# One rotation of eight PSUM banks, and another order of products and output matmuls, in an attention and gMLP kernel

## The chip, the cores and the metric

The kernel runs on one core of a Trainium2 chip. The metric is device time in microseconds for one execution. TensorE multiplies matrices into PSUM, which has eight banks. VectorE, ScalarE and GpSimd do the work between the matmuls, and SyncE's queue issues the DMA transfers.

## The reference

Three parts follow one another. Attention with a causal window of 128 over 4 batches, 8 heads, 576 positions and head size 64 gives `x`. A gated MLP with a spatial gate turns `x` into a new `x`, and a gated linear unit with a depthwise convolution ends it.

```python
scores = scale * q @ k.T + bias          # window 128, slopes by head
attn = exp(scores - max) / sum           # then attn @ v -> x [4, 576, 512]

h = gelu(x @ w_in)                       # 512 -> 1024
u, v = h[..., :512], h[..., 512:]
v_n = (v - mean) / sqrt(var + 1e-6) * g_ln
v_s = einsum('ts,bsd->btd', w_sg, v_n) + b_sg
x = x + (u * v_s) @ w_out                # spatial gate, back to 512

h = relu(x @ w_in)
gate = sigmoid(depthwise_conv(h, 3))
return (h * gate) @ w_out
```

## The kernel before

The program is one string of steps, built by `_steps()`, and each step is a function that emits instructions on several engines. A tile scheduler then orders each engine's queue by these steps, and a planner (`pick`, `book`, the table `load`) chooses for each piece of helper work the engine that it expects to be free first. TensorE's work in the two middle parts runs through the helper `mm` (L213), transpositions through L515.

Batches 0 to 2 run in a software pipeline: while the gMLP of batch b is computed, the attention of batch b + 1 is worked in between. In one such round come first the V and U steps of batch b (`psv`, `psu`: the matmuls with `w_in`), and then the second half of the round, which the change touches. Its steps, where p counts pairs of heads of the next batch:

- `C` scores of a pair (`sc`, five PSUM banks), `E` the score additions on VectorE (L451, tiles `t`, `st`) and the exponentials on ScalarE (L186), nine of each, `N` the reciprocal `r` of the sums (L498, L499) and nine norms (L242).
- `T` thirteen transpositions of a pair's weights into four banks (`pT`) and their copies to `ph` (L222 on ScalarE, L224 on VectorE), `A` 52 matmuls of the products with V (`o`), `X` the copies of the products to `x` and their two-part split into `xg`.
- `G` the spatial gate: 14 matmuls `pss` for each of eight groups, the eviction `t` (L840, VectorE), the product with `u` (L231, GpSimd) and the split into `gh` and `gl`.
- `W` the output matmuls `pso`, 12 for each of eight groups, with the sum `x` of `pso` and the old `x` (L231), which is stored to `x2d` by SyncE (L859). The buffers of the eviction `t` and of this stored sum come from one pool, so either can wait for a store to land.
- `a` pieces of narrowing a later weight (`wa`, L324 to L331, `wh`), woven into batches 1 and 2.

Each of the names `T`, `A`, `G[0]` (256 columns), `G[1]` (320 columns), `W[0]`, `W[1]` in the code is a list with one entry for each pair or group, and `gw` is the order of the second half. PSUM's eight banks are two pools until batch 3: two banks for all `ps` names except `pT` (the network) and six for `sc`, `pT` and `o` (attention); the helper `bank` takes the next in turn. The function `one_rotation` makes one pool of all eight; it is a step named `B`, which before doesn't use. Batch 3 and the last part have banks of their own.

Of the kernel before, what the change touches and what calls it, by code (L numbers as in the profile page):

```python
# [14 lines left out]
B, H, S, D = 4, 8, 576, 64  # L15
# [38 lines left out]
def _steps():  # L54


    def of(p):
        return f"{p // NP}.{p % NP}"

    def scores(p):  # L60
        return [f"C{of(p)}"]

    def weigh(p):
        return [f"E{of(p)}", f"N{of(p)}"]
# [4 lines left out]
    def halves(p):  # L69
        return [f"X{of(p)}.0", f"X{of(p)}.1"]  # L70

    def loads(p):
        return [f"L{of(p)}", f"M{of(p)}"]
# [5 lines left out]
    s = """  # L79
# [6 lines left out]
    for b in range(B - 1):  # L86
        p = NP * (b + 1)
        V = [f"V{b}.{j}" for j in range(5)]
        U = [[f"U{b}.{half}.{m}" for m in range(4)] for half in range(2)]
        G = [[f"G{b}.{half}.{m}" for m in range(4)] for half in range(2)]  # L90
        W = [[f"W{b}.{half}.{m}" for m in range(4)] for half in range(2)]
        if b == 0:
            uv = ["g0", "g1", V[2], "g2", "o0.0", U[0][3], "g3", "o0.1", V[4]] + loads(p) + ["g4", "o1.0"] + scores(p) + ["o1.1", V[3], "o2.0", "o2.1"]
            uv += loads(p + 1) + U[1][:2] + ["o3.0"] + scores(p + 1) + ["o3.1"] + loads(p + 2) + U[1][2:] + scores(p + 2)
        else:
            uv = V[:2] + loads(p) + scores(p) + V[2:] + loads(p + 1) + scores(p + 1) + U[0] + loads(p + 2) + U[1][:1] + scores(p + 2) + U[1][1:]
        T, A = ([f"{x}{of(p + i)}" for i in range(4)] for x in "TA")
        gw = weigh(p) + G[0] + weigh(p + 1) + G[1][:1] + loads(p + 3) + T[:1] + G[1][1:2] + W[0][:1] + A[:1] + halves(p)
        gw += weigh(p + 2) + W[0][1:2] + T[1:2] + W[0][2:] + A[1:2] + scores(p + 3) + halves(p + 1) + weigh(p + 3) + T[2:3] + G[1][2:3]
        gw += A[2:3] + halves(p + 2) + G[1][3:] + T[3:] + W[1][:1] + A[3:] + halves(p + 3) + W[1][1:]  # L100
        if b == 0:
            s += uv + gw
        else:
            now = put_by[10 * b - 10 : 10 * b]
            s += weave(uv, now[:4]) + weave(gw, now[4:])
# [11 lines left out]
    s = weave(n[:-6], put_by[LATE:]) + n[-6:]  # L117
    late = [f"w1.{k}.{h}" for k in range(4) for h in range(2)]
    s = s[:-6] + weave(s[-6:], late)
# [996 lines left out]
```

## Time and profile before

| what | us |
|---|---|
| median of 3 runs | 545.88 |
| lowest and highest run | 544.2, 546.34 |
| the profiled execution | 545.05 |
| its span | 543.2 |
| TensorE busy in it | 522.3 |
| VectorE busy | 370.0 |
| ScalarE busy | 258.6 |
| GpSimd busy | 243.0 |

The span runs from the first to the last instruction. Of the profiled span, 82 to 126.1 is about the second half of batch 0's round, 126.1 to 157.3 the V and U steps of batch 1, 157.3 to 205.5 batch 1's second half, 205.5 to 238 batch 2's V and U steps, 238 to 284.9 its second half; batch 3 and the last part follow. A row of a timeline reads: start, length, engine, line, operation, result and operands, count, and in brackets the idle time ahead of it and what ended it. TensorE's rows overlap a little, since its matmuls are pipelined. "PEclk" is the share of TensorE's full clock that was granted.

### The profile page before, as it was taken

The numbers are of one execution on the slowest core, as the hardware profiler recorded it, in microseconds if no ns is written. First come the engines' busy times: TensorE is split into PE (matmuls) and PEld (weight loads), VectorE is DVE, ScalarE is ACT, GpSimd is POOL, SyncE is SP. The second block draws the span as 40 slices with busy tenths as digits, with TensorE's granted clock in tenths as the row PEclk, the third lists the DMA queues.
The fourth block names the chain that finished last, engine by engine and source line by source line (L and its number), as shares of the span: only waits on it lengthen the run. The fifth ranks groups of instructions, "written<-read, shape, count | busy, mean of one in ns | idle before, by whom it ended". The sixth has DMA issues, their size and how long they took to land.

```text
span 543.2 us, 11985 instructions
## 1 busy us (share of the span) xinstructions
PE 522.3 (96%) x4548; PEld 474.8 (87%) x4548; DVE 370.0 (68%) x959; ACT 258.6 (48%) x673; POOL 243.0 (45%) x383
## 2 busy tenths in 40 slices
PE   8997989999999999999999999999999999999997
PEld 6776879898898888898988999998998999999887
DVE  4999898754869865869867788698467344654300
ACT  6694578342458451457544534453444334444311
POOL 2444249552246263237363354245586445465500
PEclk9999989999999999999999999999999999999999
DMA  8974441433260766240734424811202200100111
GB/s 298 385 241 172 150 126 45 146 120 106 80 194 21 229 183 198 68 136 24 241 124 131 154 80 155 306 43 43 83 21 69 77 21 19 42 21 22 37 39 59
DMA packets 33209, 63.93 MB, mean 118 GB/s; under 512 B 3968, under 2 KB 13952, under 8 KB 33152
## 3 DMA queue, kind: packets, MB, share of 16 engines
q1 hardware_dynamic: 33008, 63.04, 35.0%
q8 instruction: 36, 0.59, 0.4%
q14 instruction: 21, 0.17, 0.1%
q10 hardware_dynamic: 144, 0.13, 0.1%
HBM read 48.47 MB, written 14.68 MB: 116 GB/s over the span
## 4 chain that ended last, share of the span: by engine, by line
PE 57%; DVE 17%; ACT 11%; POOL 8%; DMA 3%; issue 3%; ACTq 0%; POOLq 0%; DVEq 0%; SPq 0%
PE psg L213 31%; PE pso L213 7%; PE psu L213 5%; ACT t L186 5%; PE psv L213 4%; PE o L213 3%; PE sc L213 3%; POOL t L242 3%; PE pss L213 3%; DVE t L451 2%; PE pT L515 2%; DMA x2d<-x 2%; DVE t L242 1%; DVE wa L330 1%; DVE wa L329 1%
## 5 line engine op out<-in xcount | busy, mean ns | idle before, releaser
L213 PEld LDWEIGHTS psg<-x2g,w 128*128 128x128 f32 x768 | 103.2, 188 | 2.4 <-ACT hb L970 0.7
L213 PE MATMUL psg<-x2g,w 128*128 128x256 f32 (+1 forms) x768 | 104.7, 294 | 0.6 <-ACT hb L970 0.5
L213 PE MATMUL psg<-wout,gh 128*128 128x512 f32 (+1 forms) x272 | 80.1, 378 | 0.0
L186 ACT ACTIVATE t<-t,st 128x192 f32<-128x192 f32 (+1 forms) x144 | 61.9, 431 | 16.6 <-DVE st L451 16.6
L213 PE MATMUL pss<-wsg,vn 128*128 128x256 f32 (+1 forms) x448 | 63.6, 299 | 0.3 <-DVE t L840 0.2
L213 PEld LDWEIGHTS pss<-wsg,vn 128*128 128x128 f32 x448 | 60.7, 191 | 1.2 <-DVE t L840 1.1
L974 DVE SCALAR_TENSOR_TENSOR cc<-hb,cw,cc 128x576 f32<-128x576 f32 x32 | 26.5, 832 | 47.0 <-POOL cc L242 47.0
L213 PEld LDWEIGHTS psg<-wout,gh 128*128 128x128 f32 x272 | 49.7, 188 | 8.7
L213 PE MATMUL psu<-xg,win 128*128 128x320 f32 (+1 forms) x384 | 54.4, 298 | 3.0 <-ACT win L222 1.7
L213 PEld LDWEIGHTS psu<-xg,win 128*128 128x128 f32 x384 | 51.6, 188 | 4.3 <-ACT win L222 1.8
L213 PE MATMUL pso<-gh,wo 128*128 128x256 f32 (+1 forms) x256 | 52.2, 300 | 1.7 <-DVE t L840 1.6
L213 PE MATMUL psg<-wout,gl 128*128 128x512 f32 (+1 forms) x136 | 50.9, 378 | 0.0
L213 PE MATMUL psv<-win,xg 128*128 128x512 f32 x192 | 47.6, 398 | 1.0 <-DVE wa L328 0.9
L242 POOL TENSOR_SCALAR cc<-hb,cw 128x576 f32<-128x576 f32 x32 | 28.4, 889 | 42.7 <-ACT hb L970 42.7
L451 DVE CUSTOM_DVE_ANT_0 t<-sc,tab 128x192 f32<-128x192 f32 (+1 forms) x144 | 40.3, 335 | 4.9 <-PE sc L213 4.9
L970 ACT ACTIVATE hb<-psg 128x576 f32<-128x576 f32 x32 | 20.7, 651 | 47.5 <-PE psg L213 45.1
L213 PEld LDWEIGHTS pso<-gh,wo 128*128 128x128 f32 x256 | 40.2, 188 | 3.4 <-DVE t L840 2.8
L213 PEld LDWEIGHTS psv<-win,xg 128*128 128x128 f32 x192 | 35.4, 188 | 8.9 <-ACT win L222 1.0
L231 DVE TENSOR_TENSOR gg<-cc,hb 128x576 f32<-128x576 f32 x32 | 30.2, 944 | 17.2 <-ACT cc L186 17.0
L213 PE MATMUL pso<-gl,wo 128*128 128x256 f32 (+1 forms) x128 | 36.9, 301 | 2.4 <-DVE gl L231 1.7
L231 POOL TENSOR_TENSOR t<-t,u 128x256 f32<-128x256 f32 (+1 forms) x32 | 27.0, 850 | 21.3 <-DVE t L840 20.3
L231 POOL TENSOR_TENSOR gl<-gg,gh 128x512 fp32r<-128x512 f32 x24 | 33.7, 1406 | 0.6
(101 smaller groups left out, 963.1 us busy)
## 6 DMA issues: line engine op xcount, KB each, us to landing
V<-in_v_dram SPq DMA_DIRECT2D x12, 704.0 KB, 5.1
x2s<-x2d SPq DMA_DIRECT2D x16, 288.0 KB, 2.9
w<-in_w_in_dram SPq DMA_DIRECT2D x8, 512.0 KB, 7.4
w<-in_w_out_dram SPq DMA_DIRECT2D x16, 256.0 KB, 2.9
w<-in_w_in_dram SPq DMA_DIRECT2D x16, 256.0 KB, 2.7
wout<-w2d SPq DMA_DIRECT2D x8, 512.0 KB, 6.1
q<-in_q_dram SPq DMA_DIRECT2D x12, 320.0 KB, 3.9
out_dram<-ot SPq DMA_DIRECT2D x15, 256.0 KB, 2.0
```

Of the source, the lines that this page charges most:

```text
L186: ins = nc.scalar.activation(*args, **kw)
L213: return nc.tensor.matmul(out, lhsT, rhs, start=start, stop=stop, **kw)
L231: return (nc.vector if eng == "dve" else nc.gpsimd).tensor_tensor(dst, a, b, op=op)
L242: e.tensor_scalar(dst, src, col, 1.0, op0=ALU.mult, op1=ALU.mult)
L329: nc.vector.tensor_scalar(a, a, 0x07FFFFFF, 3, op0=ALU.bitwise_and, op1=ALU.logical_shift_left)
L330: nc.vector.scalar_tensor_tensor(a, high, 0xC0000000, a, op0=ALU.bitwise_and, op1=ALU.bitwise_or)
L451: nc.vector.tensor_tensor_reduce(e, bank, table, scale=-SCALE, scalar=3e38, op0=ALU.add, op1=ALU.min, accum_out=mx)
L515: grouped(nc.tensor.transpose(ps[:, i * P : (i + 1) * P], src, ident), first and i == 0, waits if i == 0 else ())
L970: nc.scalar.activation(h[:, 1 : S + 1], ps[:, 256 : 256 + S], AF.Relu)
L974: nc.vector.scalar_tensor_tensor(cc, h[:, 0:S], cw[:, 0, c : c + 1], cc, op0=ALU.mult, op1=ALU.add)
```

## The change

A step `B` is put after batch 0's V and U steps, so all eight banks form one rotation from batch 0's second half to batch 2. And `gw` is written anew: the first group of `pso` (`W[0][:1]`) goes from ahead of the first pair's products to behind the third pair's weights (`weigh(p + 2)`), so that the products (`A[:1]`) follow `pss` directly; the third transpositions (`T[2:3]`) go ahead of the last scores, and their products ahead of the last two groups of `pss` instead of behind the first of them; the last group of `W[0]` goes from ahead of the last scores to behind these `pss` groups; the last weights (`weigh(p + 3)`) go behind the third products. The first three lines of `gw` stay in the code, overwritten.

```diff
--- before.py
+++ after.py
@@ -98,8 +98,12 @@
         gw = weigh(p) + G[0] + weigh(p + 1) + G[1][:1] + loads(p + 3) + T[:1] + G[1][1:2] + W[0][:1] + A[:1] + halves(p)
         gw += weigh(p + 2) + W[0][1:2] + T[1:2] + W[0][2:] + A[1:2] + scores(p + 3) + halves(p + 1) + weigh(p + 3) + T[2:3] + G[1][2:3]
         gw += A[2:3] + halves(p + 2) + G[1][3:] + T[3:] + W[1][:1] + A[3:] + halves(p + 3) + W[1][1:]
+        if True:
+            gw = weigh(p) + G[0] + weigh(p + 1) + G[1][:1] + loads(p + 3) + T[:1] + G[1][1:2] + A[:1] + halves(p)
+            gw += weigh(p + 2) + W[0][:1] + T[1:2] + W[0][1:2] + A[1:2] + halves(p + 1) + T[2:3] + W[0][2:3] + scores(p + 3)
+            gw += A[2:3] + halves(p + 2) + weigh(p + 3) + G[1][2:] + W[0][3:] + T[3:] + W[1][:1] + A[3:] + halves(p + 3) + W[1][1:]
         if b == 0:
-            s += uv + gw
+            s += uv + ["B"] + gw
         else:
             now = put_by[10 * b - 10 : 10 * b]
             s += weave(uv, now[:4]) + weave(gw, now[4:])
```

In after all line numbers behind the diff are higher by four (L217 for L213, L519 for L515, L844 for L840).

The first place is TensorE's queue in batch 1, at the first pair's products `o`. Before:

```order
L213 MATMUL pso<-gh,wo 128x256 x2
L213 MATMUL pso<-gl,wo 128x256
L213 MATMUL o<-ph,V 64x64 x4
L213 MATMUL o<-ph,V 64x192 x2
L213 MATMUL o<-ph,V 64x64 x16
L213 MATMUL o<-ph,V 64x128 x2
L213 MATMUL o<-ph,V 64x64 x2
L515 MATMUL pT<-ident,t_86 128x128 x13
L213 MATMUL pso<-gh,wo 128x256 x2
```

After:

```order
L217 MATMUL pss<-wsg_851,vn 128x320 x2
L217 MATMUL pss<-wsg_852,vn 128x320
L217 MATMUL o<-ph,V 64x64 x4
L217 MATMUL o<-ph,V 64x192 x2
L217 MATMUL o<-ph,V 64x64 x16
L217 MATMUL o<-ph,V 64x128 x2
L217 MATMUL o<-ph,V 64x64 x2
L217 MATMUL pso<-gh,wo 128x256
L519 MATMUL pT<-ident,t_86 128x128 x13
```

Before, 18 matmuls `pso` stand between the last `pss` of this group and the products; after, the products follow `pss`, and the rest of that `pso` group stands behind the second transpositions.

The second place is TensorE's queue in batch 1 behind the last scores `sc`. Before:

```order
L213 MATMUL sc<-k,q 64x128 x2
L213 MATMUL sc<-k,q 64x64 x2
L213 MATMUL sc<-k,q 128x192
L213 MATMUL pss<-wsg_851,vn 128x320
L213 MATMUL pss<-wsg_852,vn 128x320
L213 MATMUL pss<-wsg_851,vn 128x320 x2
```

After:

```order
L217 MATMUL sc<-k,q 64x64 x2
L217 MATMUL sc<-k,q 128x192
L217 MATMUL o<-ph,V 64x64 x4
L217 MATMUL o<-ph,V 64x192 x2
L217 MATMUL o<-ph,V 64x64 x16
L217 MATMUL o<-ph,V 64x128 x2
L217 MATMUL o<-ph,V 64x64 x2
L217 MATMUL pss<-wsg_851,vn 128x320
L217 MATMUL pss<-wsg_852,vn 128x320
```

The third pair's products, which in before follow 28 `pss`, a transposition and 16 `pso`, now stand directly behind the scores; their transpositions have gone ahead of 12 `pso` and the scores.

The third place is VectorE's queue in batch 1, at the last pair's reciprocal `r` and norms (`t_87`), where the two evictions `t` of the last `pss` groups stand. Before:

```order
L451 ISA st_91 128x1
L840 SCALAR_TENSOR_TENSOR t_2890<-pss,gln,bsg 128x320
L498 TENSOR_SCALAR r<-st_91 128x9
L499 RECIPROCAL r<-r 128x9
L242 TENSOR_SCALAR t_87<-t_87,r 128x192
L324 TENSOR_SCALAR wa<-w_2837 128x256
L328 TENSOR_SCALAR wa<-wa 128x256
L840 SCALAR_TENSOR_TENSOR t_2949<-pss,gln,bsg 128x320
```

After:

```order
L503 RECIPROCAL r<-r 128x9
L332 TENSOR_SCALAR wa<-wa 128x256
L235 TENSOR_TENSOR xg<-x,xg 128x320
L246 TENSOR_SCALAR t_87<-t_87,r 128x192 x3
L333 TENSOR_SCALAR wa<-wa 128x256
L246 TENSOR_SCALAR t_87<-t_87,r 128x192
L844 SCALAR_TENSOR_TENSOR t_2916<-pss,gln,bsg 128x320
L334 SCALAR_TENSOR_TENSOR wa<-w_2864,wa 128x256
L335 SCALAR_TENSOR_TENSOR wa<-w_2864,wa 128x256
L844 SCALAR_TENSOR_TENSOR t_2938<-pss,gln,bsg 128x320
L235 TENSOR_TENSOR gl<-t_2514,gh 128x320
```

The first eviction stood ahead of the reciprocal and the second behind one norm; now both stand behind all the norms that VectorE does of this pair.

## Rows read from the trace of the kernel before

**Rows 1.** Batch 1's second half: start:end, length, busy time by engine, clock, DMA.

```profile
core 0: us, PE busy (x) PEld busy (x) DVE busy (x) ACT busy (x) POOL busy (x), PEclk, DMA share, GB/s
157.30:205.50 48.20, 45.11 (x516) 42.59 (x515) 36.46 (x110) 29.69 (x102) 25.18 (x46) 1.00 0.51 158
```

**Rows 2.** TensorE in batch 1: start, length, operation, count, idle time before it.

```profile
169.79 0.41 PE L213 MATMUL pso<-gh,wo 128*128 128x256 f32 x2
...
171.54 0.38 PE L213 MATMUL pso<-gl,wo 128*128 128x256 f32 x1 [0.64 <-DVE gl L231]
172.20 0.50 PE L213 MATMUL pso<-gh,wo 128*128 128x256 f32 x2 [0.28 <-DVE t L840]
...
173.44 2.05 PE L213 MATMUL o<-ph,V 128*64 128x64 f32 x52
...
177.96 2.04 PE L213 MATMUL o<-ph,V 128*64 128x64 f32 x52 [0.21 <-ACT ph L222]
```

**Rows 3.** TensorE's timeline in the last third of batch 1's half.

```profile
189.63 1.61 PE L515 MATMUL pT<-ident,t 128*128 128x128 f32 x13 [0.62 <-DVE st L451]
...
192.85 0.56 PE L213 MATMUL pso<-gh,wo 128*128 128x320 f32 x2 [0.43 <-DVE t L840]
...
194.94 2.04 PE L213 MATMUL o<-ph,V 128*64 128x64 f32 x52 [0.66 <-issue]
...
199.91 2.04 PE L213 MATMUL o<-ph,V 128*64 128x64 f32 x52 [0.18 <-ACT ph L222]
```

**Rows 4.** ScalarE's timeline, from the table load to the two copies.

```profile
157.98 1.28 ACT L186 ACT_TABLE_LOAD   x1
...
171.14 1.04 ACT L222 COPY ph<-pT 128x512 f32<-128x512 f32 x2
```

**Rows 5.** VectorE's timeline in batch 1's half.

```profile
176.59 1.28 DVE L224 COPY ph<-pT 128x512 f32<-128x512 f32 x2
...
178.18 0.41 DVE L231 TENSOR_TENSOR x<-pso,x 128x256 f32<-128x256 f32 x1
...
184.16 0.42 DVE L231 TENSOR_TENSOR x<-pso,x 128x256 f32<-128x256 f32 x1 [1.40 <-DMA x2d<-x]
...
192.25 0.55 DVE L840 SCALAR_TENSOR_TENSOR t<-pss,gln,bsg 128x320 f32<-128x320 f32 x1
```

**Rows 6.** GpSimd's timeline, two rows of batch 0 and one of batch 1.

```profile
95.03 1.80 POOL L242 TENSOR_SCALAR t<-t,r 128x128 f32<-128x128 f32 x4
96.80 2.55 POOL L231 TENSOR_TENSOR gl<-t,gh 128x256 fp32r<-128x256 f32 x3
...
196.14 0.86 POOL L231 TENSOR_TENSOR t<-t,u 128x320 f32<-128x320 f32 x1
```

**Rows 7.** TensorE's timeline, in batch 0 and in batch 2.

```profile
96.65 0.50 PE L213 MATMUL pso<-gh,wo 128*128 128x256 f32 x2 [0.63 <-DVE t L840]
...
219.00 2.09 PE L213 MATMUL psv<-win,xt 128*128 128x512 f32 x8 [0.43 <-ACT v L186]
...
226.17 1.53 PE L213 MATMUL psu<-xg,win 128*128 128x256 f32 x11 [0.45 <-ACT u L186]
...
250.40 0.40 PE L213 MATMUL pso<-gh,wo 128*128 128x256 f32 x2
...
284.91 2.45 PE L213 MATMUL psv<-win,xg 128*128 128x512 f32 x10
```

**Rows 8.** Two early stretches, columns as in rows 1.

```profile
46.00:52.00 6.00, 3.29 (x49) 2.83 (x48) 5.86 (x13) 3.50 (x9) 1.45 (x2) 1.00 0.10 38
77.50:80.50 3.00, 3.00 (x21) 2.88 (x16) 2.97 (x15) 3.00 (x15) 0.64 (x1) 0.50 0.14 41
```

**Rows 9.** TensorE's timeline ahead of and in these stretches.

```profile
47.86 1.37 PE L213 MATMUL o<-ph,zin 128*64 128x64 f32 x36 [1.01 <-ACT ph L222]
50.93 0.39 PE L213 MATMUL psu<-xg,win 128*128 128x256 f32 x1 [1.70 <-ACT win L222]
...
76.79 2.20 PE L213 MATMUL sc<-k,q 64*64 64x192 f32 x24 [2.08 <-DVE st L451]
```

## The prediction

> **What bounds the kernel now.** I read the stages first. TensorE is busy for 45.11 of the 48.20 us of batch 1's second half [rows 1], and the other engines for much less, so the change can only win or lose through TensorE's idle time. The list of what TensorE waits for comes next, then its timeline at each wait, and last the timeline of whichever engine ended it. In the part that the change touches there are four kinds of wait. (a) The first `pso` block of a batch waits 0.64 for the last `gl` and 0.28 for the eviction that frees one of the two network banks [rows 2]. (b) The second pair's products wait 0.21 for a copied `ph` [rows 2]. (c) The last third of the half waits 0.62 for the score additions to free a bank, 0.43 for an eviction, 0.66 marked "issue" and 0.18 for a `ph` [rows 3]. (d) Batch 2's V and U stage waits 0.43 and 0.45 for banks that ScalarE still reads, and batch 0's first `pso` waits 0.63 for an eviction [rows 7]. Batch 2 repeats (a), (b), the 0.66 and the 0.18. All of it comes to about 6.5 us, 1.2% of the time, which is the most that eight banks and a perfect order could give.
>
> **Parts that cost nothing.** The change adds and removes no work on TensorE: the same 3,754 instructions stand on its queue, in another order, and from batch 3's first `psv` on the blocks follow one another as before. On the helpers some pieces change engine, for example about ten more norm scalings on VectorE and ten fewer on GpSimd. VectorE, ScalarE and GpSimd all have idle time in each stage [rows 1], so these moves count only where TensorE waits behind them, and there I count them below.
>
> **The banks.** With eight banks in one rotation a bank comes back after seven others. In batch 2's V and U stage the two waits of 0.43 and 0.45 are waits for a bank's last reader [rows 7]; eight tiles back that reader has long finished. They go, and I put the gain at 0.9. The bounds are 0 (what is computed next from `v` and `u` is late anyway) and 0.9. Batch 1's V stage shows no such wait, so it gains nothing.
>
> **The first products of batches 1 and 2.** Here the new order costs time, and the price can be read almost without an estimate. In before the sixth `pss` group ends at 169.79, 18 `pso` matmuls fill the time up to 173.44, and then the first pair's products start without a wait [rows 2]. Now these products follow `pss` directly. They need four copies `ph`, two of which ScalarE makes. ScalarE loads its table at 157.98 and then works without a gap through 27 exponentials to those two copies, which run from 171.14 to 172.18 [rows 4]. Its order up to there is the same in both kernels, and the banks don't hold it: it is bound by its own work. So TensorE reaches the products at 169.8 and starts them at 172.2: **an idle time of 2.4 us in place of 0.64 + 0.28**. In batch 2 `pss` ends at 250.40 [rows 7], and the same two copies there stand at the same distance, so 2.4 again.
>
> TensorE then has: products to 174.2, one `pso` matmul and the second transpositions to 175.8, 23 `pso` matmuls to 178.6. The second pair's products need two `ph` copies on VectorE. In before these begin at 176.59 and end at 177.78 [rows 5]. Now one more norm (about 0.3) and two weight pieces (0.3 each) stand ahead of or between them, and the addition for `xg` moves in between; I get 179.3, so a wait of 0.7. The bounds are 0 and 0.8. At this point of equal work before stood at 177.96 [rows 2]: **batch 1 is 1.3 us late**.
>
> **From there to the next V stage.** Before takes 205.50 − 177.96 = 27.54 [rows 1, 2], of which 0.62 + 0.43 + 0.66 + 0.18 = 1.89 are waits [rows 3]. Behind each wait the pipeline starts anew (a pair of matmuls takes 0.50 at 172.20, against 0.41 at 169.79 [rows 2]); with some 0.14 for each of four the bare work is some 25.1. Without any wait batch 1 would end at 204.4, 1.1 early. I don't expect that, for two reasons.
>
> First, the third `pso` result is now stored ahead of the score additions of the last pair on VectorE. Its buffer must be free, that is, an earlier store must have landed. In before such a store stands at 184.16 with a wait of 1.40 for the transfer [rows 5], 6.0 us behind the addition at 178.18 that wrote what is being stored. In after the store it waits for is written at about 180.0, so with 4.3 to 5.7 us for the way (an estimate: somewhat less than that one row, which has the addition itself in it) the buffer is free between 184.3 and 185.7. The nine additions, nine exponentials on ScalarE (0.44 each, as the 27 between 159.26 and 171.14 [rows 4], with a copy among them) and the norms follow, which end at 192.9 to 194.3. TensorE comes to the last transpositions at 193.5: a wait of 0 to 0.8.
>
> Second, the two `pss` evictions (L840 of before), of which one ran ahead of the reciprocal and the other at 192.25, behind one norm [rows 5], now both stand behind the last norms. Behind them hang GpSimd's product `t`·`u` (0.86 [rows 6]), the cast `gh`, the difference `gl`, and on VectorE the `ph` copies of the last pair. Following that chain from 192.9 or 194.3, TensorE waits in the eleven `pso` matmuls of 320 columns and again at the last products: 0.9 at the early end, 1.5 at the late end, restarts counted.
>
> So batch 1 ends at 179.3 + 25.1 + 0.9 = 205.3 to 179.3 + 25.1 + 2.3 = 206.7, against 205.50: −0.2 to +1.2, middle +0.5. (2.3 is the late end's 0.8 + 1.5.) Batch 2 follows the same order; its `pss` ends 80.61 later (250.40 − 169.79 [rows 2, 7]), so its end is 285.9 to 287.3 against 284.91 [rows 7]: +1.0 to +2.4, middle +1.7. It is worse because before has fewer waits there to lose.
>
> **Batch 0's second half.** The products need GpSimd's `gl` pieces: three stand from 96.80 on, 2.55 us, behind four norms of 1.80 [rows 6]. Now there are five norms, so the last `gl` comes at about 99.7 instead of 99.35. The `pso` work is three matmuls' worth further ahead, so TensorE waits longer in between, 2.2 us in place of 1.2, and ends the second group 0.1 late. The rest adds waits of 0 to 0.5 at the last transpositions and products. Sum +0.1 to +0.6, middle +0.35. The third transpositions, moved ahead, cost nothing: their norms are long done.
>
> **Sum.** +0.35 (batch 0) + 0.5 (batch 1) − 0.9 (V and U) + 1.7 (batch 2) = +1.65, ends 0.0 and +3.3. The profiled execution took 545.05, 0.83 under the median of 545.88; the sum is made on the first and carried to the second: **547.5**, and 545.9 to 549.2 for this case alone.
>
> **TensorE's clock.** The 2.08 us of idle time ahead of 76.79 are followed by three microseconds at a granted clock of 0.50, the lower of the two levels (1.2 of 2.4 GHz), from 77.5 to 80.5; yet in 46 to 52, where TensorE is idle for 1.01 and 1.70 us, the clock stays at 1.00 [rows 8, 9]. The new idle times of 2.4 lie between these. A fall of that length costs about 1.7 us of work; the 0.7 us that TensorE then waits for the second `ph` would take part of it, which leaves 0.9 or so for each batch.
>
> The Trainium skill, page "TensorE: Matmul & The Clock Gate", section "A second HAM failure mode: psum-queue depth-cycling", speaks against this change: it tells of a kernel that cycles through PSUM banks, whose TensorE idles briefly between groups of matmuls, and whose clock swings between the two levels for it. By that rule the fall after each first pair would be the likely case and the time 549.3. The trace agrees in one stall of 2.08 us and disagrees in the pair of 1.01 and 1.70.
>
> **Rivals.**
> 1. *The clock falls behind both new idle times.* +1.8 on top of the sum, 549.3, and up to 551 with the late ends. For it: the stall of 2.08 us is the nearest single row. Against it: 46 to 52. It decides if the granted clock is below 1 for over 2 us behind both. Chance 0.25.
> 2. *The tails run without waits.* If the stores land early and the evictions keep up, batch 1 ends 1.1 early, batch 2 0.1 late, V and U gain 0.9, batch 0 loses 0.1: −1.8, time 544.1; if the second pair doesn't wait for its `ph` either, 0.7 less in each batch, 542.7. For it: eight banks free the evictions from their deadline. Against it: the chains run over data, not over banks. Chance 0.2.
> 3. *The banks do nothing.* The waits in V and U stay as waits for ScalarE's results; +0.9, time 548.4. Nothing else in the sum rests on the banks. Chance 0.05.
>
> **How the numbers follow.** The forecast has 0.5. Half a per cent, 2.7 us, is about what a measurement of this kernel can tell from no change: 543.2 to 548.6. Of the forecast's case 0.07 lies above that, of rival 1 nearly all 0.23, of rival 3 0.01; of rival 2 about half, 0.10, lies below. So faster 0.10, same 0.59, slower 0.31. The range leaves out the upper part of rival 1 and the lower part of rival 2: 543.5 to 550.3.
>
> **What would show it.** After's trace should have TensorE idle for 2.2 to 2.6 us ahead of the first products `o` of batches 1 and 2, ended by ScalarE's `ph`; about 0.7 ahead of the second; no wait at batch 2's `psv` and `psu`; a wait for `gl` of batch 0's first `pso` in GpSimd's name; and waits on `gh`, `gl` or `ph` in the last third. The granted clock in the 4 us behind the two long idle times separates the forecast from rival 1. I would be wrong from the root if the first products didn't wait, which would need ScalarE's copies 2 us earlier, and wrong in the tail if batch 1's half were shorter than 47 us or longer than 50.

## The result, and the profile after

The changed kernel takes **553.75 us** (median of 6 runs, 551.1 to 558.29) against 546.11 for the kernel before, measured beside it (6 runs, 544.2 to 548.9): a ratio of **1.0143, with 95% interval 1.0097 to 1.019**. The kernel is slower by 7.6 us, where I forecast a loss of 1.65 that could hardly be told from none, and the time lies above the range. The profiled execution of after took 553.90, with a span of 552.1 against 543.2 before.

By stage, from the starts of the stages on TensorE in the two timelines:

| stretch | before, us | after, us | change | forecast |
|---|---|---|---|---|
| up to batch 0's end | 126.10 | 126.50 | +0.40 | +0.35 |
| batch 1, V and U | 31.20 | 31.20 | 0 | 0 |
| batch 1, second half | 48.20 | 49.82 | +1.62 | +0.5 |
| batch 2, V and U | 32.45 | 31.22 | −1.23 | −0.9 |
| batch 2, second half | 46.96 | 52.11 | +5.15 | +1.7 |
| batch 3 and the last part | 258.29 | 261.25 | +2.96 | 0 |
| sum | 543.2 | 552.1 | +8.90 | +1.65 |

The busy times on the page of after: engine, us busy, share of the span, instructions.

```profile
PE 522.3 (95%) x4548; PEld 474.1 (86%) x4548; DVE 381.0 (69%) x977; ACT 256.6 (46%) x667; POOL 237.3 (43%) x371
```

TensorE is as busy as in before (522.3 on both pages, which count 4,548 matmuls each, not the 3,754 that I named), so all of the 8.9 is idle time. A fall of the clock lengthens the busy time, and each of the two profiled executions holds one, at another place: before in batch 0's round [rows 8], after in batch 2. VectorE has 18 instructions and 11.0 us more than in before (x959, 370.0), ScalarE and GpSimd less. The windows of the two second halves (as in [rows 1]; batch 1, then batch 2):

```profile
157.70:207.52 49.82, 44.94 (x516) 42.52 (x515) 41.29 (x117) 28.73 (x99) 22.81 (x40) 1.00 0.51 151
...
238.74:290.85 52.11, 46.66 (x516) 44.08 (x515) 43.41 (x131) 28.73 (x99) 23.69 (x42) 0.97 0.39 118
```

VectorE is now busy for 41.29 of 49.82 us where it was 36.46 of 48.20 [rows 1]. TensorE in batch 1 of after, the rows that answer to [rows 2, 3]:

```profile
172.63 2.04 PE L217 MATMUL o<-ph,V 128*64 128x64 f32 x52 [2.62 <-ACT ph L226]
...
180.26 2.04 PE L217 MATMUL o<-ph,V 128*64 128x64 f32 x52 [1.22 <-issue]
...
197.67 0.41 PE L217 MATMUL pso<-gl,wo 128*128 128x320 f32 x1 [0.38 <-DVE gl L235]
198.44 0.56 PE L217 MATMUL pso<-gh,wo 128*128 128x320 f32 x2 [0.36 <-DVE gh L228]
199.17 0.41 PE L217 MATMUL pso<-gl,wo 128*128 128x320 f32 x1 [0.17 <-DVE gl L235]
```

The first products wait 2.62 for ScalarE's `ph`, as forecast (2.4). The second wait 1.22 (forecast 0.7); the row says "issue", which means that the profile shows nothing that it waited for, but VectorE's second copy `ph` ends just ahead of it, at 180.15. In the last third the waits for `gh` and `gl` stand where I put them; the wait at the last transpositions (0 to 0.8) didn't come. In batch 2 the same places read:

```profile
248.25 1.64 PE L519 MATMUL pT<-ident,t 128*128 128x128 f32 x13 [0.70 <-POOL t L246]
253.68 2.04 PE L217 MATMUL o<-ph,V 128*64 128x64 f32 x52 [1.75 <-ACT ph L226]
...
262.25 2.81 PE L217 MATMUL o<-ph,V 128*64 128x64 f32 x52 [1.94 <-issue]
264.99 2.45 PE L519 MATMUL pT<-ident,t 128*128 128x128 f32 x13
```

Here the first transpositions wait 0.70 for GpSimd's norms, which they don't in batch 1, and the second products wait 1.94. Behind these the clock falls: the products take 2.81 instead of 2.04, and the transpositions 2.45 instead of 1.64. The windows:

```profile
262.20:264.50 2.30, 2.25 (x48) 2.28 (x50) 2.27 (x7) 0.41 (x1) 1.18 (x2) 0.74 0.52 165
264.50:265.50 1.00, 1.00 (x11) 0.88 (x8) 0.96 (x4) 0.40 (x1) 0.10 (x1) 0.50 0.69 192
265.50:268.00 2.50, 2.50 (x19) 2.50 (x18) 1.30 (x4) 1.46 (x4) 1.14 (x2) 0.76 0.93 247
```

A granted clock of 0.50 is the lower level. Products and transpositions lose 0.77 + 0.81 = 1.58 us: the starts are 2.74 and 2.21 apart, against 1.97 and 1.40 in batch 1.

Batch 0's round differs more than its +0.40 says. First the windows from 76.5 to 81, before and after, then three rows of TensorE in after:

```profile
76.50:81.00 4.50, 4.21 (x36) 4.13 (x37) 4.47 (x26) 4.50 (x21) 1.14 (x2) 0.62 0.42 135
```

```profile
76.50:81.00 4.50, 3.16 (x39) 2.94 (x40) 4.46 (x26) 4.50 (x21) 1.30 (x2) 1.00 0.42 125
```

```profile
80.91 5.33 PE L217 MATMUL pss<-wsg,vn 128*128 128x256 f32 x43 [1.23 <-DVE st L455]
87.23 1.64 PE L519 MATMUL pT<-ident,t 128*128 128x128 f32 x13 [0.99 <-POOL t L246]
...
101.19 2.04 PE L217 MATMUL o<-ph,V 128*64 128x64 f32 x52 [0.22 <-DVE ph L228]
```

The clock that fell in before stays at 1.00 in after, though the wait ahead of it is the same (2.09 against 2.08). In its place come two waits that I hadn't forecast: `pss` waits 1.23 for the score additions, which still read the bank that it takes in the common rotation, and the first transpositions wait 0.99 for GpSimd's norms.

### The profile page after: what moved, and what is told of

The parts are those of the page before. It is cut to its first block, busy times and chain, and to the rows that moved or that the text cites. A ratio compares the mean times of both kernels' runs of the same rounds, so it can differ in the third digit from the quotient of the medians.

```text
span 552.1 us, 11995 instructions
## 1 busy us (share of the span) xinstructions
PE 522.3 (95%) x4548; PEld 474.1 (86%) x4548; DVE 381.0 (69%) x977; ACT 256.6 (46%) x667; POOL 237.3 (43%) x371
## 4 chain that ended last, share of the span: by engine, by line
PE 65%; DVE 13%; ACT 10%; POOL 6%; issue 3%; DMA 2%; SPq 0%; ACTq 0%; POOLq 0%; DVEq 0%
PE psg L217 30%; PE pso L217 8%; PE psv L217 7%; ACT t L190 6%; PE psu L217 5%; PE o L217 5%; PE pss L217 3%; PE sc L217 3%; PE pT L519 2%; POOL t L246 2%; DVE t L455 2%; DVE wa L334 1%; DVE gg L235 1%; DVE cc L978 1%; DVE wa L333 1%
## 5 line engine op out<-in xcount | busy, mean ns | idle before, releaser
L217 PEld LDWEIGHTS psg<-x2g,w 128*128 128x128 f32 x768 | 103.0, 188 | 3.7 <-POOL x2g L229 1.0
L217 PE MATMUL psg<-x2g,w 128*128 128x256 f32 (+1 forms) x768 | 105.0, 294 | 1.2 <-ACT hb L974 0.5
L217 PE MATMUL psg<-wout,gh 128*128 128x512 f32 (+1 forms) x272 | 80.3, 378 | 0.2 <-ACT gh L226 0.2
L217 PE MATMUL pss<-wsg,vn 128*128 128x256 f32 (+1 forms) x448 | 61.9, 295 | 1.2 <-DVE st L455 1.2
L217 PEld LDWEIGHTS pss<-wsg,vn 128*128 128x128 f32 x448 | 59.5, 188 | 1.6 <-issue 1.4
L217 PEld LDWEIGHTS psg<-wout,gh 128*128 128x128 f32 x272 | 49.5, 188 | 9.1 <-ACT gh L226 0.7
L217 PE MATMUL psu<-xg,win 128*128 128x320 f32 (+1 forms) x384 | 54.2, 298 | 2.6 <-ACT win L226 1.7
L217 PEld LDWEIGHTS psu<-xg,win 128*128 128x128 f32 x384 | 51.7, 188 | 3.7 <-ACT win L226 1.8
L217 PE MATMUL pso<-gh,wo 128*128 128x256 f32 (+1 forms) x256 | 52.4, 299 | 0.7 <-DVE gh L228 0.7
L217 PE MATMUL psg<-wout,gl 128*128 128x512 f32 (+1 forms) x136 | 51.1, 378 | 0.0
L217 PE MATMUL psv<-win,xg 128*128 128x512 f32 x192 | 47.7, 398 | 1.0 <-DVE wa L332 0.9
L217 PEld LDWEIGHTS psv<-win,xg 128*128 128x128 f32 x192 | 35.4, 188 | 8.9 <-ACT win L226 1.0
L217 PEld LDWEIGHTS pso<-gh,wo 128*128 128x128 f32 x256 | 40.7, 188 | 1.6 <-DVE gh L228 1.2
L217 PE MATMUL pso<-gl,wo 128*128 128x256 f32 (+1 forms) x128 | 37.9, 307 | 3.6 <-DVE gl L235 2.6
```

The costliest lines, as they stand in the source:

```text
L217: return nc.tensor.matmul(out, lhsT, rhs, start=start, stop=stop, **kw)
```

## The experiments

I held against each other: that the loss is the new idle time ahead of the first products; that it is the eight banks themselves; that VectorE's queue makes the second products late; and that the new order of the last third loses it. Each diff is against the kernel after; a line that a diff of several kernels shares is shown once, and lines of `gw` with + alone stand in place of those of after. Medians are set beside the kernel before on the same chip (544.97 to 546.14).

**The banks alone, with the old steps.**

```
-        if True:
+        if False:
             gw = weigh(p) + G[0] + weigh(p + 1) + G[1][:1] + loads(p + 3) + T[:1] + G[1][1:2] + A[:1] + halves(p)
```

> The step B of the change alone, with the order of steps of before. TensorE's queue has 9 pso matmuls ahead of the first products of batches 1 and 2 instead of 18, since the scheduler sees other banks. Theory 1: idle about 1.4 ahead of these products, V and U of batch 2 quicker by 1.2, time 546 to 549. Theory 2 (the tail of the new order): 544 to 546, since the new tail is not in it. Theory 3 (the banks): 551 to 554.

Measured: 560.68, ratio 1.0284 (1.0228 to 1.0341), the slowest of all. TensorE's rows with the longest waits:

```profile
198.01 2.83 PE L519 MATMUL pT<-ident,t 128*128 128x128 f32 x13 [4.21 <-ACT t L190]
...
281.75 3.01 PE L519 MATMUL pT<-ident,t 128*128 128x128 f32 x13 [4.08 <-ACT t L190]
```

With eight banks the scheduler, which sees a bank for each tile, puts the third transpositions right behind their scores; TensorE then waits 4.2 us for ScalarE's exponentials. So here the pools act mainly through the order that is written on TensorE's queue, not through waits for banks.

**The new steps alone, with the old pools.**

```
         if b == 0:
-            s += uv + ["B"] + gw
+            s += uv + gw
```

> The new order of steps without B, so two banks for the network and six for attention. TensorE's queue has 18 pso matmuls ahead of the first products again, and the third transpositions early. Theory 1: no idle time of over 0.7 us at the first products, time 545 to 548. Theory 2 (the tail of the new order, with the third transpositions early): 550 or more. Theory 3 (the banks): 545 to 546.

Measured: 550.55, 1.0107 (1.0052 to 1.0163). With two network banks 18 `pso` matmuls stand ahead of the first products again, and no wait of 2.62 is there. The second products wait 1.67 and 1.69, the last transpositions 1.00 in batch 1, the last products 0.61. So in the medians more than half of the loss (5.3 of 7.6 us) comes without the first idle time and without eight banks. The V and U steps of batch 2 take 31.22 us here too (207.53 to 238.75), without a wait and without eight banks.

**The first `pso` back ahead of the first products**, one block of nine matmuls in the first kernel, two in the second.

```
-            gw = weigh(p) + G[0] + weigh(p + 1) + G[1][:1] + loads(p + 3) + T[:1] + G[1][1:2] + A[:1] + halves(p)
-            gw += weigh(p + 2) + W[0][:1] + T[1:2] + W[0][1:2] + A[1:2] + halves(p + 1) + T[2:3] + W[0][2:3] + scores(p + 3)
+            gw = weigh(p) + G[0] + weigh(p + 1) + G[1][:1] + loads(p + 3) + T[:1] + G[1][1:2] + W[0][:1] + A[:1] + halves(p)
+            gw += weigh(p + 2) + T[1:2] + W[0][1:2] + A[1:2] + halves(p + 1) + T[2:3] + W[0][2:3] + scores(p + 3)
```

> As after, but one group of pso ahead of the first products; by the order of TensorE's queue 9 pso matmuls, some 1.0 us, fill the idle time there in batches 1 and 2. Theory 1: the idle time shrinks from 2.6 to about 1.5 and the time lies between: 548 to 551. Theories 2 and 3: 551 to 554.

> Eight banks and the rest of the new order, but two groups of pso stand ahead of the first pair's products, so that in batches 1 and 2 TensorE again has 18 pso matmuls there, as in before. Theory 1 (the loss is the idle time of 2.6 and 1.75 us ahead of the first products, what it does to the second products, 1.22 and 1.94, and the clock's fall behind it): these idle times shrink below 0.5 each, the clock stays at 1.00 in batch 2, time 546 to 548.5. Theory 2 (the loss is in the tail, from the third transpositions to the last pso, which is unchanged here): the time stays at 551 to 554. Theory 3 (the eight banks themselves, which put other work behind other waits): also 551 to 554.

Measured: 553.82, 1.0153 (1.011 to 1.0196), and 555.21, 1.0178 (1.0125 to 1.0231). The first products' wait goes from 2.62 to 0.33 (and 0.98 in the `pso` block ahead of them) and to 0.22, and nothing is gained: the second products wait 1.56 in the one and 3.01 in the other. In e5 all four copies of the second pair stand on VectorE, the last until 184.07, while ScalarE is idle for 6.23 us. The theory that the first idle time is the loss fell.

**Nearly the order of before on eight banks, and there the second pair's copies on ScalarE.** Behind the third transpositions stand 9 `pso` matmuls where before has 16. The steps of e10, and the edit that e11 has beside them:

```
+            gw = weigh(p) + G[0] + weigh(p + 1) + G[1][:1] + loads(p + 3) + T[:1] + G[1][1:2] + W[0][:2] + A[:1] + halves(p)
+            gw += weigh(p + 2) + T[1:2] + A[1:2] + halves(p + 1) + W[0][2:] + scores(p + 3) + weigh(p + 3) + G[1][2:] + T[2:3] + W[1][:1]
+            gw += A[2:3] + halves(p + 2) + T[3:] + W[1][1:2] + A[3:] + halves(p + 3) + W[1][2:]
...
-            pc = turned(tails(t) + [other(t, 3), other(t, 2)], first=True, waits=masks)
-            p1 = turned([whole(t, 1, i) for i in range(4)])
-            last = pick(dict(act=640, dve=740))
+            pc = turned(tails(t) + [other(t, 3), other(t, 2)], "act" if b >= 2 and m == 1 else "act dve", first=True, waits=masks)
+            p1 = turned([whole(t, 1, i) for i in range(4)], "act" if b >= 2 and m == 1 else "act dve")
+            last = "act" if b >= 2 and m == 1 else pick(dict(act=640, dve=740))
```

> Eight banks, with the steps written so that TensorE's queue has nearly the order of before: 18 pso ahead of the first products, the third transpositions behind the last 28 pss (9 pso of 320 columns behind them instead of 16). The planner still gives all second ph copies to VectorE, as in the run of two pso groups first. Theory 4: the second products wait about 3 us in each round and the clock falls there; 551 to 555. Theory 2 (the new tail costs): 545 to 547, since the tail is before's. Theory 3 in its narrow form (eight banks cost at run time, whatever the order): 552 or more, but with the waits on banks.

> The run before it in this list, with the second ph copies on ScalarE. Theory 4: no wait of over 0.5 us at the second products, V and U of batch 2 quicker by 1.2 as in the changed kernel; 544 to 547, about the time of before. Theory 3 in its narrow form: 551 or more.

Measured: e10 549.22, 1.006 (1.0033 to 1.0087); e11 **546.2, 1.0008 (0.9987 to 1.003)**. The second products of batch 1, e10 and then e11:

```profile
180.35 2.04 PE L217 MATMUL o<-ph,V 128*64 128x64 f32 x52 [3.01 <-issue]
```

```profile
177.65 2.04 PE L217 MATMUL o<-ph,V 128*64 128x64 f32 x52 [0.17 <-ACT ph L226]
...
189.77 1.64 PE L519 MATMUL pT<-ident,t 128*128 128x128 f32 x13 [1.04 <-DVE st L455]
194.28 0.41 PE L217 MATMUL pso<-gl,wo 128*128 128x320 f32 x1 [1.70 <-DVE gl L235]
...
205.96 5.67 PE L217 MATMUL psv<-win,xg 128*128 128x512 f32 x24
```

A wait of 3.01 in e10 is 0.17 in e11, and 3.0 us come back. As a whole eight banks cost nothing and bring nothing with this order: e11's profiled execution gains 1.22 in the V and U steps of batch 2 (31.23 against 32.45), but is 0.6 late at batch 0's end (126.71) and 0.8 longer from batch 3 on (259.10 against 258.29). What costs 3.0 in e10 is that the planner, after the steps changed, put all four copies of the second pair on VectorE (177.78 to 180.25), behind its norms and `gl`; before and after have two of them there.

**The same move of the copies in the kernel after, and in e5.** The diff is the lower part of the one above.

> The changed kernel with the same single edit: the second pair's ph copies on ScalarE in the rounds of batches 1 and 2. Theory 4: the first products' idle time of 2.6 and 1.75 stays, the second products' 1.22 and 1.94 goes, so does the fall of the clock behind it; 549 to 551. Theory 3: 553 or more.

> The run with two pso groups first (555.2), with one more edit: the ph copies of the second pair of batches 2 and 3 (worked in the rounds of batches 1 and 2) all go to ScalarE. In that run VectorE held them behind its norms, casts and xg, TensorE waited 3.0 us for them in each round while ScalarE had nothing to do for 6.2 us, and the granted clock fell behind each wait. Theory 4 (VectorE's queue sets when the second products start): the second products wait under 0.5 us, no fall behind them, time 546 to 549. Theory 3 (eight banks cost by themselves): the waits move elsewhere, 553 or more.

Measured: e8 550.76, 1.0113 (1.0049 to 1.0176); e7 555.75, 1.0178 (1.0142 to 1.0213). In e8 the second products don't wait at all, the first still wait 2.61, and the median is 3.0 us under after's, though the two intervals overlap. In e7 the gain of the second products is lost again in the last third: the scores wait 0.80 for a `ph`, the last transpositions 1.13 and the `pso` matmuls 0.66, 0.36, 0.36 and 0.17. It was no gain there.

**The first edit alone, with the old last third, on eight banks**; e14 is the same with the second pair's copies on ScalarE.

```
-            gw += weigh(p + 2) + W[0][:1] + T[1:2] + W[0][1:2] + A[1:2] + halves(p + 1) + T[2:3] + W[0][2:3] + scores(p + 3)
-            gw += A[2:3] + halves(p + 2) + weigh(p + 3) + G[1][2:] + W[0][3:] + T[3:] + W[1][:1] + A[3:] + halves(p + 3) + W[1][1:]
+            gw += weigh(p + 2) + W[0][:1] + T[1:2] + W[0][1:2] + A[1:2] + halves(p + 1) + W[0][2:] + scores(p + 3) + weigh(p + 3) + G[1][2:] + T[2:3] + W[1][:1]
+            gw += A[2:3] + halves(p + 2) + T[3:] + W[1][1:2] + A[3:] + halves(p + 3) + W[1][2:]
```

> Eight banks and the first edit of the order alone: the first products ahead of all pso, and from the second products on the order of before (third transpositions behind the last pss). Against the changed kernel only the tail differs. Theory 5 (the new tail puts VectorE's queue late and costs 3 to 5 us, part of it in batch 3 and after): 548.5 to 551. Its rival (all of the loss lies ahead of the second products, in waits for VectorE's ph): 553 to 555, as the changed kernel.

> The run before it in this list, with the second pair's ph copies on ScalarE. Compared with the run that has 18 pso ahead of the first products, the order of before and the same copies (546.2), only the idle time ahead of the first products, 2.6 us in each of two rounds, is added and the wait for the second products not. If that idle time costs its length less the waits it replaces, about 1 us a round: 547 to 549. If it is all absorbed by the waits behind it: 546. With the clock falling behind it: 550.

Measured: e12 549.15, 1.0054 (1.0023 to 1.0085); e14 547.77, 1.0037 (1.0004 to 1.0069). TensorE in e12, batch 1 and batch 2:

```profile
172.61 2.05 PE L217 MATMUL o<-ph,V 128*64 128x64 f32 x52 [2.62 <-ACT ph L226]
180.24 2.04 PE L217 MATMUL o<-ph,V 128*64 128x64 f32 x52 [1.22 <-issue]
...
205.42 0.85 PE L217 MATMUL psv<-win,xg 128*128 128x512 f32 x3
```

```profile
251.56 2.04 PE L217 MATMUL o<-ph,V 128*64 128x64 f32 x52 [2.45 <-ACT ph L226]
258.83 2.05 PE L217 MATMUL o<-ph,V 128*64 128x64 f32 x52 [0.87 <-DVE ph L228]
```

The two waits of batch 1 are word for word those of after, at 172.61 and 180.24. From the second products to the next V stage e12 takes 205.42 − 180.24 = 25.18 us, without a wait; after takes 207.52 − 180.26 = 27.26. In batch 2 it is 25.15 (258.83 to 283.98) against 28.60 (262.25 to 290.85), of which 1.58 is the clock. The difference of 2.08 in batch 1 is therefore the new last third alone. The medians differ by 553.75 − 549.15 = 4.6 us, but they hold the clock too. In the profiled execution of e12 it never fell, and that one took 546.21. The mean granted clock of its ten executions is 0.9896, against 0.9945 for before beside it. Of some 545 us that is 2.7 (an estimate), nearly all of the 3.0 by which e12's median lies over that of before. Where those falls stand no trace shows.

**The third products behind fifteen of the `pss` matmuls**, and **the last norms off VectorE**: two attempts on the last third of the kernel after.

```
-            gw += A[2:3] + halves(p + 2) + weigh(p + 3) + G[1][2:] + W[0][3:] + T[3:] + W[1][:1] + A[3:] + halves(p + 3) + W[1][1:]
+            gw += weigh(p + 3) + G[1][2:] + A[2:3] + halves(p + 2) + W[0][3:] + T[3:] + W[1][:1] + A[3:] + halves(p + 3) + W[1][1:]
```

```
-            scaled(e, e, r[:, c : c + 1], ON["norm"])
+            scaled(e, e, r[:, c : c + 1], "act pool" if b >= 2 and m >= 2 else ON["norm"])
```

> The changed kernel with one edit: the third pair's products go back behind the first of the last two pss groups (TensorE: 15 pss, products, 13 pss), the third transpositions stay early. On VectorE the first pss eviction then stands ahead of the last pair's reciprocal and norms, as in before, and the second behind two norms. Theory 5 in its narrow form (the loss in the tail is the chain eviction, product with u, gh, gl, behind the late pss): the eleven pso of 320 columns lose less than 1 us to waits instead of 2.3, 550 to 552.5. Its rival (the tail is late because VectorE has more to do, wherever the evictions stand): 553 to 555.

> The kernel after, with the 18 norms of the third and last pair of each round no longer offered to VectorE: ScalarE and GpSimd share them. Theory A (VectorE's queue carries the loss of the last third): the eleven pso matmuls lose less than the 2.3 us of after, because the evictions and gl that stand behind those norms come sooner, batch 3's first pso no longer waits 1.07 for gl, and the time is 549.5 to 552. Rival (any helper late is as bad; the last pair's chain of exponentials, norms and transpositions is the bound): the norms take longer on the other two engines, the last transpositions wait for them by 0.5 or more, and the time is 553 to 557.

> The kernel after, with both edits: the second pair's copies ph on ScalarE (which took the second products' waits away and gave 550.8) and the norms of the third and last pair on ScalarE and GpSimd. Theory A: both gains add, the second products don't wait, the last third loses under 1.5 us a round, and the time is 546.5 to 549.5, as the kernel before. Rival: ScalarE becomes late in the last third, the transpositions wait for its norms, and the time is 551 to 556, no better than with the first edit alone.

Measured: e17 552.55, 1.0129 (1.0104 to 1.0154). The part from the last scores to the V stage is 21.87 us (187.17 to 209.04), against 22.30 in after (185.22 to 207.52) and 20.27 in e12 (185.15 to 205.42). So a fifth of the difference comes back; the interval overlaps that of after, and this run alone doesn't settle it. e18 has 555.99, 1.0203 (1.0153 to 1.0253), and e19, which also has e8's edit, 552.75, 1.0152 (1.0087 to 1.0218): in the medians both slower than without the edit (553.75 and 550.76), but not by more than their intervals. GpSimd in after and in e18, at the norms of the last pair:

```profile
191.81 2.36 POOL L246 TENSOR_SCALAR t<-t,r 128x128 f32<-128x128 f32 x5 [0.92 <-DVE r L503]
194.42 0.97 POOL L235 TENSOR_TENSOR t<-t,u 128x320 f32<-128x320 f32 x1 [0.25 <-DVE t L844]
```

```profile
192.28 4.35 POOL L246 TENSOR_SCALAR t<-t,r 128x128 f32<-128x128 f32 x8 [0.92 <-DVE r L503]
196.60 0.87 POOL L235 TENSOR_TENSOR t<-t,u 128x320 f32<-128x320 f32 x1
```

VectorE is free earlier in e18 and then waits 1.49 for GpSimd's `t`: eight norms run there instead of five, the product `t`·`u` starts 2.18 later, and TensorE's `gl` wait is 1.24. The theory that VectorE's load alone carries the last third fell; GpSimd has no room there either.

**A version that is a little faster than both.** Batch 0 as in before, eight banks only from batch 1's second half, there the order of before with the two network blocks closer together, and the second pair's copies on ScalarE as in e11:

```
-        if True:
+        if b:
+            gw = weigh(p) + G[0] + weigh(p + 1) + G[1][:1] + loads(p + 3) + T[:1] + G[1][1:2] + W[0][:2] + A[:1] + halves(p)
+            gw += weigh(p + 2) + T[1:2] + A[1:2] + halves(p + 1) + W[0][2:] + scores(p + 3) + weigh(p + 3) + G[1][2:] + T[2:3] + W[1][:2]
+            gw += A[2:3] + halves(p + 2) + T[3:] + A[3:] + halves(p + 3) + W[1][2:]
...
-            s += uv + ["B"] + gw
+            s += uv + gw
...
-            s += weave(uv, now[:4]) + weave(gw, now[4:])
+            s += weave(uv, now[:4]) + (["B"] if b == 1 else []) + weave(gw, now[4:])
```

> An attempt at a version that beats both: batch 0 as before, eight banks only from batch 1's second half, there the order of before (18 pso ahead of the first products, 18 ahead of the third) and the second ph copies on ScalarE. If eight banks can give what the V and U stage of batch 2 shows (1.2) and nothing is lost elsewhere: 543.5 to 545.5. If helpers give it back: 545.5 to 547.

Measured: **543.6, 0.9958 (0.9929 to 0.9987)**, against 546.14. It is a small gain, but its interval is clear of 1; of the fourteen kernels of this section it is the only one whose interval lies below 1. Which of its edits brings it was not separated. In its profile the second products wait 0.48 in batch 1, the last products 0.47, and the V and U stage of batch 2 has no wait.

## Why the prediction was wrong

In short: three terms of the sum failed. The wait of the second products was bounded by 0.8 us and measured 1.22 and 1.94; the last third's waits had in part a wrong cause; and the helpers beyond batch 2 were put at nothing and that part is 2.96 longer. The largest miss is batch 2's half, 1.7 forecast and 5.15 measured. Of this 1.62 is what batch 1 lost too, and 1.24 is that before's half is that much shorter there, which the forecast had. Then 0.97 is the second products' later place within the half and 1.58 the clock, and the rest is −0.26.

**Place and size of the first idle time were right, its consequence was not.** I forecast 2.4 us ahead of the first products; 2.62 and 1.75 came. I then carried the 1.3 us by which batch 1 was to be late straight to the end of the half. With the old last third that lateness is taken up: e12 has 2.62 and 1.22 of new idle time, and its half of batch 1 is 47.71 us against 48.20 before. The nearest pair is e11 and e12, whose steps are the same from the second products on: e11 starts these products at 177.65 and its next V stage at 205.96, e12 at 180.24 and 205.42. So 2.59 us of lateness cost nothing there, though some helper pieces, the copies `ph` above all, stand on other engines in e11; e11 spends them in the two waits shown above, of 1.04 for the score additions and 1.70 for `gl`. The helpers' chains set the end of this stretch, so a TensorE that arrives later waits less. In the medians e12 (549.15) equals e10 (549.22), which differs by this edit. Where the second pair's copies don't delay anything, the edit may cost: e14 less e11 is 547.77 − 546.2 = 1.6, 0.8 a round, but their intervals overlap, and in the profile of e14 the clock fell behind the first products of batch 1.

**The second products' wait was mis-sized:** 0.7 forecast, with 0.8 as the upper bound; 1.22 and 1.94 measured. The rows of VectorE in after, batch 1:

```profile
175.89 0.61 DVE L235 TENSOR_TENSOR gl<-t,gh 128x256 fp32r<-128x256 f32 x1
176.43 0.52 DVE L228 CAST gh<-t 128x320 fp32r<-128x320 f32 x1
176.87 0.95 DVE L235 TENSOR_TENSOR xg<-x,xg 128x256 fp32r<-128x256 f32 x1
177.75 0.28 DVE L328 TENSOR_SCALAR wa<-w 128x256 uint32<-128x256 uint32 x1
178.06 0.29 DVE L332 TENSOR_SCALAR wa<-wa 128x256 f32<-128x256 f32 x1
178.27 0.68 DVE L228 COPY ph<-pT 128x512 f32<-128x512 f32 x1
178.87 0.28 DVE L333 TENSOR_SCALAR wa<-wa 128x256 uint32<-128x256 uint32 x1
179.07 0.48 DVE L235 TENSOR_TENSOR xg<-x,xg 128x320 fp32r<-128x320 f32 x1
179.47 0.68 DVE L228 COPY ph<-pT 128x512 f32<-128x512 f32 x1
```

The rows are those that I had listed: a fifth norm (five end at 175.97), two weight pieces ahead of the copies and one between, and the addition for `xg` between. But `gl` takes 0.61 and the first addition for `xg` 0.95, where before has 0.41 and 0.61 for them, and the copies stand in two rows of 0.68 instead of one of 1.28 [rows 5]. The second copy ends at 180.15; 0.39 of that is the later start of the half (157.72 against 157.33), so my 179.3 was 0.46 short. In batch 2 the same rows stand 0.97 later within the half. I asked what the new rows cost on VectorE, and not whether another engine was free: ScalarE is idle from 177.10 to 181.85 in after. Giving it these copies is worth 3.0 us in e11 against e10; e8 against after has 3.0 too, within the noise, and e7 against e5 nothing.

**The last third: the place was right, and in batch 1 the size too, but this by luck.** I forecast 25.1 us of work and 0.9 to 2.3 of waits, 26.0 to 27.4; 27.26 came, at the late end. But the early stores, which I made one cause, caused no wait on the last transpositions. Without their 0.8 my bound was 1.5, and some 2.2 came. (My 0.14 for a new start behind a wait isn't that of the rows that I named, 0.50 less 0.41; the bare work was right all the same, 25.18 in e12.) From the last scores on e12 and after have nearly the same work on TensorE, and differ by 2.03 us. In e12 the third transpositions and products (3.3 us) stand behind `pss` and cover the way from the `pss` evictions over `t`·`u` and `gh` to `gl`. In after they stand ahead of it, and 12 `pso` matmuls (1.4 us) stand behind instead. So 1.9 us of cover are gone. VectorE and GpSimd can't shorten that way: the one has work from 190.88 on until the last of these `gl`, and the other got worse with three more norms (e18). That the cover is the cause is argued from these rows and not shown; e17, which put the products back behind half of `pss`, regained 0.43 of it.

**The gain in V and U came (1.23, forecast 0.9) and didn't last in after.** I took it as time saved. Batch 2's first transpositions wait 0.70 for GpSimd's norms, and the second products 1.94 instead of 1.22. That the shorter stage brings this isn't shown: in e11, e12 and e14 the stage is as short (31.23 and 31.24), and their first transpositions have no such wait. Nor do the banks alone bring the gain, since e3 has it with the old pools. These rows show ScalarE reading the banks that `psv` waited for in before; they are of before, of after and of e3:

```profile
218.26 1.08 ACT L186 ACTIVATE v<-psv 128x512 f32<-128x512 f32 x2
```

```profile
220.90 1.08 ACT L190 ACTIVATE v<-psv 128x512 f32<-128x512 f32 x2
```

```profile
218.60 0.59 ACT L190 ACTIVATE v<-psv 128x512 f32<-128x512 f32 x1
```

Counted from the stage's start (205.50, 207.52, 207.53) this is at 12.76, 13.38 and 11.07. In after ScalarE reads later than in before and TensorE doesn't wait, as I had argued from the eight banks; in e3 it reads earlier, and two banks are enough.

**Batch 0: +0.40 came for +0.35, in part by luck.** GpSimd has the fifth norm that I forecast, but its three `gl` end at 99.39, not at 99.7. TensorE reaches the second products 0.1 late (101.19 against 101.09), as forecast, with two unforeseen waits of 1.23 and 0.99 ahead, where before spends about as much on the fall of the clock.

**The part beyond batch 2, held at nothing, is 2.96 longer.** In batch 3, where the order on TensorE is that of before, its first rows of `pso` wait for VectorE:

```profile
326.81 0.39 PE L217 MATMUL pso<-gl,wo 128*128 128x256 f32 x1 [1.07 <-DVE gl L235]
...
330.15 0.62 PE L217 MATMUL pso<-gl,wo 128*128 128x256 f32 x3 [0.40 <-DVE gl L235]
```

Before has only the second of these, 0.41. On VectorE no norms stand ahead of this `gl`, but pieces of weight narrowing, for which VectorE itself waits for ScalarE ("wa"):

```profile
315.71 0.29 DVE L332 TENSOR_SCALAR wa<-wa 128x256 f32<-128x256 f32 x1 [1.71 <-ACT wa L326]
...
320.71 0.55 DVE L332 TENSOR_SCALAR wa<-wa 128x256 f32<-128x256 f32 x1 [0.46 <-ACT wa L326]
...
325.81 0.94 DVE L235 TENSOR_TENSOR gl<-t,gh 128x256 fp32r<-128x256 f32 x1
```

And e18, which takes the last pair's norms from VectorE, has 1.28 in place of 1.07. The wait goes with the new last third on eight banks (0.98 in e8, 1.15 in e17); it is 0.45 at most with the old last third (e10, e11, e12 and e14), and 0.32 in e3, with the old pools. From batch 3's first `psv` to its second group of `psg` it is 56.68 us in after (290.85 to 347.53) and 55.09 in before (284.91 to 340.00): 1.59, of which the row of 1.07 is the most. The step that failed is the sentence that pieces which change engine count only where TensorE waits behind them, and that I had counted these places: I had looked no further than batch 2. By which chain the new order makes VectorE late there stays open. The rest, some 1.4 us, is in the last part. There after has other short waits, but e11, e12 and e14 show as long a last part in faster kernels, so I can't tie it to the change. It stays open.

**The clock fell at another place than rival 1 said:** in the profile once, behind the wait of batch 2's second products and not of its first, and cost 1.58. Since before's profile holds a fall as well, the clock doesn't explain the 8.9 as a whole. In other kernels with the same wait ahead of the first products rival 1 did come true, in one round of e14 and in both of e17. Rival 3 was wrong in its own words, since the waits in V and U went; that the banks bring nothing else at run time holds for e11 as a whole, while in after `pss` waits 1.23 for a bank in batch 0. Rival 2, tails without waits, is what e12 shows, with the old last third; the new one stands in its way.

In medians 3.0 for the second pair's copies behind VectorE's queue (gone in e8 and e11) and 4.6 for the new last third (e12) make the 7.6 by which after is over before. That this closes exactly is luck: the interval of the 7.6 reaches from 5.3 to 10.4, the 4.6 hold a different clock, and the terms don't add where they are combined. With both edits, as in e14, 1.6 are left over before, and not nothing. So the second products' wait and the new last third are shown as places of the loss, by e11 against e10 (with the old last third) and by e12 against after; their exact shares are not.

## What to carry to other kernels

A wait that is new on the busiest engine is not a loss until one knows whether a later stretch is bound by the helpers: it may be taken up there, and a gain may not last. When work is moved ahead, ask what it covered where it stood (here this is argued, not shown), and count the way from the last eviction to the first use of its result against the work that is left between. When a planner gives out work, look in the new order for every copy that changed its engine and what is queued ahead of it, and move it by hand to the engine that is idle.

## What the runs showed of the hardware

**The clock did not follow the length of the wait ahead of it.** A single idle time of TensorE of 4.21 and 4.08 (e2) and of 1.94 (after, batch 2) was followed by a fall, one of 3.01 fell in e5 and not in e10's batch 1, and one of 2.62 fell in e14's batch 1 (the first products take 3.28) and not in after's or e12's. The Trainium skill, page "TensorE: Matmul & The Clock Gate", section "A second HAM failure mode: psum-queue depth-cycling", tells of a kernel that cycles through PSUM banks, whose TensorE idles briefly and often between groups of matmuls, and whose clock swings for it. No such effect of the rotation shows here: e11 has eight banks in rotation and no idle time of over 0.4 us ahead of the first and second products of batches 1 and 2, and the mean granted clock of its ten executions is 0.995, against 0.996 for before beside it. e12 has the same rotation with idle times of 2.62, 1.22, 2.45 and 0.87; its profiled execution has 1.000, the other nine 0.984 to 0.994. So in these two kernels a lower clock goes with the idle times and not with the rotation, and not in every execution.

**A fall can also come and go in code that no edit touches.** The pair of idle times at 46 to 52 [rows 9] is in every kernel. In before and after the clock stays at 1.00 there; in the profile of e13 it doesn't:

```profile
52.11 0.58 PE L217 MATMUL psu<-xg,win 128*128 128x256 f32 x1 [1.71 <-ACT win L226]
...
59.79 0.39 PE L217 MATMUL psu<-xg,win 128*128 128x256 f32 x1 [0.53 <-ACT u L190]
```

The way between the two is 7.68 us there and 4.93 in after (50.76 to 55.69). This is some 2.7 us that come and go in the same code, as much as half a per cent, and a single profile can carry it or not.
